# A new order of the prologue of an attention-plus-MLP kernel, and two pieces of h summed by TensorE

## The chip, the cores and the metric

The kernel runs on one core of one Trainium2 chip. The metric is the device time of one execution in microseconds (us): before the change a median of 589.53 us over 3 runs (589.42 to 589.62). Lower is better.

The engines are named as in the profile: PE is TensorE, DVE is VectorE, ACT is ScalarE, POOL is GpSimd and SP is SyncE, which issues DMAs here.

## The reference

```python
# x (4, 12480, 128), inducing (32, 128), w_in (128, 2048), w_out (2048, 128), alpha (2048)
def mab(q, kv):
    s = scale * (q @ kv.transpose(0, 2, 1))        # scale = 1 / sqrt(128)
    s = s - s.max(-1, keepdims=True)
    a = np.exp(s)
    a /= a.sum(-1, keepdims=True) + 1e-09
    return a @ kv
h = mab(I, x)                  # 32 inducing points look at the 12480 rows of a batch
y = mab(x, h)                  # each row looks at the 32 rows of h
...
hid = y.reshape(49920, 128) @ w_in
g = np.maximum(hid, 0.0) + alpha * np.minimum(hid, 0.0)
return g @ w_out
```

## The kernel before

The second attention and the MLP are folded: `g` is a relu part, whose weights are `W1 = w_out * (1 - alpha)`, and a linear part with a weight of its own, `Amat`. A *visit* handles 512 rows of x and 512 of the 2048 hidden columns in groups of matmuls: L855 multiplies the attention weights `a` of the rows by `HW = h @ w_in`, DVE (L870) and ACT (L868) take the relu into `gt`, and L881 multiplies `gt` by `W1`. Visits fill the program from the end of the prologue to its end. What DVE, ACT and POOL do beside them (the first attention of the next batches among it) is laid out by a planner with costs and due times, `Plan`.

The **prologue** is the first attention of batch 0, which nothing overlaps, since the first visit needs its h. It works on *pieces* of x, numbered 0 to 7: pieces 0 and 2 to 5 are loads of 1024 KB (16 tiles of 128 rows), piece 1 is the 192 rows that are left over, and pieces 6 and 7 are the two halves, 512 KB each, of the last 2048 rows. Its order is written out by hand, as one string of steps that are run from left to right; each engine's queue is in the order in which the steps issue to it. A step is a letter, a piece, a part after a point, and the engine as the last letter (p POOL, a ACT, v DVE):

- `k` casts a part of a load to bf16 (L353 on ACT, L355 on POOL and DVE), `t` transposes it on PE (L370), `c` copies the transposed tiles out of PSUM (L376 ACT, L378 DVE). When the last cast of a load has been issued, `load_next` sends the next load of x from SP.
- `s` are the scores against the inducing points on PE (L385), `m` their least value on DVE (L424; the scores carry a minus sign), `e` the exponentials on ACT (L450), `u` and `v` their transposition on PE (L488) and the copy back (L494 ACT, L496 DVE).
- `h` is a piece's share of h, summed in PSUM by PE (L505); `g` adds it to the running sum `hs` on DVE, pieces 1 to 3 with a factor `fac` (`f`, L468; L530), pieces 4 to 7 with a worth `ex` (L521).
- The tail: `ml` the lowest of all (`lo`, L399), `mg` (L549, ACT), `lz` (L406), `ex` (L584, ACT), `rb` on PE, `mm` (L565), `gs` scales `hs` (L412, POOL), `dx` and `dn` the denominator (L594, L597), `mf` the factors that join the four groups of partitions (L571), `pd` the denominator on PE (L614), `rec` its reciprocal (L619, L620), `ph` the sum of `hs` over the groups on PE (L629), `hT` the product (L634). Then `b` and the steps up to `ba` make the first attention weights `a` (L691 to L834), `w` and `hw` make `HW` (L645, L652), `kwp` casts w_in and `ww` makes `W1` and `AW` on POOL (L1137, L1021, L1030). `lw` loads w_in and w_out.
- `Z` and `W` are matmuls of blank tiles into a PSUM bank that nobody reads (L1007): one of 512 columns in f32, or so many of 256 columns in bf16.

A f32 matmul counts as several records in the profile. `al` is a small f32 transposition of alpha on PE (L1094).

Of the kernel before, what the change touches and what calls it, by code (L numbers as in the profile page):

```python
# [13 lines left out]
COPY = mybir.ActivationFunctionType.Copy  # L14
MULT = mybir.AluOpType.mult
# [6 lines left out]
P = 128  # L22
R = 4
# [3 lines left out]
EPS = 1e-9  # L27
# [3 lines left out]
def kernel(  # L31
# [9 lines left out]
    nc = tc.nc  # L41
    f32 = mybir.dt.float32
    bf16 = mybir.dt.bfloat16

    B, N, C = x.shape
    M = inducing.shape[0]
# [5 lines left out]
    scale = 1.0 / math.sqrt(C)  # L52
# [42 lines left out]
    const = ctx.enter_context(tc.tile_pool(name="const", bufs=1))  # L95
# [6 lines left out]
    sm_pool = ctx.enter_context(tc.tile_pool(name="sm", bufs=2))  # L102
# [11 lines left out]
    class Plan:  # L114
# [5 lines left out]
        COPY = {"a": 482, "v": 607}  # L120
# [164 lines left out]
    small = ring  # L285
# [9 lines left out]
    def new_state(b):  # L295
        st = State()
        st.b = b
        st.pieces = whole_pieces if b else first_pieces
        st.np = len(st.pieces)
        st.xT = xt_pool.tile([C, NT, P], bf16, name="xT", tag="xT")  # L300
        st.xn, st.xs, st.s1, st.e1T, st.e1, st.s1p, st.hp = {}, {}, {}, {}, {}, {}, {}
        st.e2, st.m2, st.den2, st.rc, st.rep = {}, {}, {}, {}, {}

        st.mx = sm_pool.tile([P, NX], f32, name="mx", tag="mx")
        st.rm = sm_pool.tile([P, NX], f32, name="rm", tag="rm")
        st.fac = sm_pool.tile([P, NX], f32, name="fac", tag="fac")
        st.da = sm_pool.tile([P, NX], f32, name="da", tag="da")
        st.ex = sm_pool.tile([P, NX], f32, name="ex", tag="ex")
        st.dx = sm_pool.tile([P, NX], f32, name="dx", tag="dx")
        st.lo = sm_pool.tile([P, 1], f32, name="lo", tag="lo") if not b else st.rm[:, st.np - 1 : st.np]  # L310
        st.den = sm_pool.tile([P, 1], f32, name="den", tag="den")
        st.hs = h_pool.tile([P, C], f32, name="hs", tag="hs")
        eng = nc.gpsimd if b else nc.vector
        eng.memset(st.mx[:], HIGH)
        eng.memset(st.da[:], 0.0)
        return st
# [198 lines left out]
    def a_add(st, pc):  # L515
# [22 lines left out]

        plan.then(work)

    def a_h_add(st, pc):
        a_h(st, pc)
        a_add(st, pc)

    def a_max(st):

        st.mg = sm_pool.tile([P, R], f32, name="mg", tag="mg")
        def work():
            nc.scalar.activation(  # L549
                out=st.mg[:], in_=group[:], func=COPY, scale=st.lo[:]  # L550
            )

        plan.then(work)

    def a_factors_pe(st):

# [52 lines left out]

    def a_den_pe(st):  # L610

        pd = small([P, M])
        den = st.den[:].broadcast_to([P, P])
        nc.tensor.matmul(pd[:], den, st.mf[:], start=True, stop=True)  # L614
        return pd

    def a_den_rec(st, pd):
        st.rec = sm_pool.tile([P, M], f32, name="rec", tag="rec")
        nc.vector.tensor_scalar(out=st.rec[:], in0=pd[:], scalar1=EPS, scalar2=None, op0=ADD)  # L619
        nc.vector.reciprocal(out=st.rec[:], in_=st.rec[:])  # L620

# [3 lines left out]

    def a_sum_pe(st):

        ph = small([P, M])
        nc.tensor.matmul(ph[:], st.hs[:], st.mf[:], start=True, stop=True)  # L629
        return ph  # L630

    def a_sum_div(st, ph):
        st.hT = hTs[st.b]
# [324 lines left out]
    st = new_state(0)  # L958
    xs_left = const.tile([P, supers[-1][1], C], f32, name="xs_left")
    for pc in first_pieces[:5]:  # L960
# [18 lines left out]
    mask = const.tile([P, M], f32, name="mask")  # L979
    nc.vector.tensor_reduce(  # L980
        out=mask[:], in_=ident32[:].rearrange("k (g m) -> k m g", g=R), axis=AX, op=ADD
    )
    group = const.tile([P, R], f32, name="group")
    nc.vector.tensor_reduce(
        out=group[:], in_=ident32[:].rearrange("k (g m) -> k g m", g=R), axis=AX, op=ADD
    )
    same = const.tile([P, R, M], f32, name="same")
    nc.vector.tensor_copy(out=same[:], in_=mask[:].unsqueeze(1).broadcast_to([P, R, M]))
    low = const.tile([P, M], f32, name="low")
    nc.vector.tensor_scalar(  # L990
        out=low[:], in0=mask[:], scalar1=-1.0, scalar2=HIGH, op0=ADD, op1=MULT
# [5 lines left out]
    W1 = const.tile([P, NK, C], bf16, name="W1")  # L997
# [72 lines left out]
    def load_next(done):  # L1070


        if not waiting:
            return
        for pc in waiting.pop(0):
            a_load(st, pc)
# [20 lines left out]
    def begin(step):  # L1097


        if step == "Z":  # L1100
            warm(blank, 1, BT * P)
            return
        if step[0] == "W":
            warm(blank_b, int(step[1:]), 2 * P)
            return
        plain = {
            "mg": lambda: a_max(st),
            "rb": lambda: kept.update(rb=a_factors_pe(st)),
            "mm": lambda: a_factors_min(st, kept["rb"]),
            "mf": lambda: a_factors_exp(st),  # L1110
            "ex": lambda: a_worth(st),
            "ml": lambda: a_lowest(st),
            "lz": lambda: a_from_lowest(st),
            "gs": lambda: a_scale(st),
            "lw": load_weights,
            "dx": lambda: a_weigh(st, nc.gpsimd),
            "dn": lambda: a_den_total(st),
            "ww": second_weights,
            "pd": lambda: kept.update(pd=a_den_pe(st)),
            "rec": lambda: a_den_rec(st, kept["pd"]),  # L1120
            "ph": lambda: kept.update(ph=a_sum_pe(st)),
            "hT": lambda: a_sum_div(st, kept["ph"]),
            "b": first_products,
            "bm": first_most,
            "bs": first_less,
            "be": lambda: b_exp_once(kept["be"], BT, w0[:, :BT]),
            "rx": rest_most,
            "rl": lambda: rest_less(BT, BT),
            "rk": lambda: rest_less(H, H),
            "re": lambda: rest_exp(BT, BT),  # L1130
            "bt": lambda: kept.update(bt=b_turn_pe(w0[:, :BT], BT)),
            "ba": lambda: b_turn_copy(st, 0, 0, BT, kept["bt"], False),
            "b2": lambda: b_products(st, 0, BT, ST - BT, later),
            "w": lambda: a_w(st),
            "al": lambda: kept.update(al=alpha_turn()),
            "alc": lambda: nc.vector.tensor_copy(out=alT[:], in_=kept["al"][:]),
            "kwp": lambda: nc.gpsimd.tensor_copy(out=w_in_b[:], in_=kept["w_in"][:]),  # L1137
            "om": lambda: nc.gpsimd.tensor_scalar(
                out=om_al[:], in0=alT[:], scalar1=-1.0, scalar2=1.0, op0=MULT, op1=ADD
            ),  # L1140
            "hw": lambda: a_w_copy(st),
            "hwv": lambda: a_w_copy(st, False),
        }
        if step in plain:
            plain[step]()
            return
        f, act = step[0], step[-1] == "a"
        p, _, part = step[1:].rstrip("avp").partition(".")
        pc = first_pieces[int(p)]
        if f in "tc":  # L1150
            t0, n = cuts[pc.n][int(part)]
            if f == "t":
                kept["t", p, part] = a_turn_pe(st, pc, t0, n)
            else:
                a_turn_copy(st, pc, t0, n, kept.pop(("t", p, part)), act)
        elif f == "k":
            a_cast_part(st, pc, *cuts[pc.n][int(part)], step[-1])
            done = first_pieces[int(p)].s
            if pc.full and step == last_cast[done]:
                load_next(done)  # L1160
        elif f == "u":
            kept["u", p] = a_e1_pe(st, pc)
        elif f == "v":
            a_e1_copy(st, pc, kept.pop(("u", p)), act)
        else:
            {"s": a_scores, "m": a_least, "e": a_exp, "f": a_fac, "h": a_h, "g": a_add}[f](st, pc)
# [5 lines left out]
    }  # L1172
    assert ST == 16 and NX == 8 and short[2] == 2
    order = """
        k0.0v k1.0p k0.1a k0.2a k2.0p Z t0.1 c0.1a t0.0 k2.2p t0.2 al k3.0p t1.0 c0.0v k2.1a
        c0.2v k3.1p Z s0 t2.1 c1.0a t2.0 alc m0 c2.0v t2.2 om c2.1v k4.0p s1 k5.2p m1 e0
        c2.2a k3.2a e1 f1 s2 t3.2 k5.0p m2 c3.2v u0 e2 t3.0 k6.0p u2 c3.0v v0v u1 v2v k4.1a
        k6.1p t3.1 t4.1 W2 t4.0 k4.2a c3.1v k7.1p f2 v1v t4.2 c4.1v c4.2v s3 m3 h0 c4.0a
        k5.1a W2 s4 e3 t5.2 g0 m4 h2 h1 g1 t5.1 t5.0 c5.2a W1 t6.0 g2 u3 k7.0p c5.1a c5.0v
        e4 W1 t6.1 s5 t7.1 v3v W1 t7.0 c6.0a c6.1v m5 f3 c7.0v s6 c7.1a m6 W2 s7 u4 e5 m7 u5  # L1180
        ml v4v e6 lw lz h3 mg ex u6 g3 v5v h4 gs e7 g4 rb dx u7 mm v6a h5 v7a mf dn h6 h7 g5
        g6 g7 pd W5 ph rec hT W4 b b2 kwp bm w bs rx be rl hw W3 bt ww ba re rk
    """
    waiting = [first_pieces[5:6], first_pieces[6:]]
    last_cast = {}
# [59 lines left out]
    first = {}  # L1245
# [61 lines left out]
    for b in range(B - 1):  # L1307
# [3 lines left out]
        for p, pc in enumerate(whole_pieces):  # L1311
# [18 lines left out]
            f = pc.full  # L1330
# [101 lines left out]
```

## Time and profile before

| what | value |
|---|---|
| median of 3 runs | 589.53 us (589.42 to 589.62) |
| the profiled execution | 591.3 us |
| its span in the profile | 589.2 us |
| PE, DVE, ACT, POOL busy | 580.1, 532.4, 538.1, 216.8 us |
| first visit begins (first L855) | 31.00 us |
| DMA moved | 80.55 MB |

The profiled execution took 2.1 us more than its span and 1.8 us more than the median. All times inside an execution below are of that one, in us from the start of its span.

### The profile page before, as it was taken

The page shows a single profiled execution, that of the slowest core. Times are in us where ns is not written, and L with a number is a line of the kernel's source. Part 1 is how long each engine was busy: PE and PEld are TensorE (multiplying, and loading weights), DVE is VectorE, ACT ScalarE, POOL GpSimd, SP SyncE. Part 2 cuts the span into 40 slices and gives each one's busy share as a digit, 9 for nine tenths or more (in the row PEclk, how much of TensorE's full clock was granted, in tenths as well). Part 3 has the DMA queues.
Part 4 walks back from the last instruction along what each step waited for, and adds up shares of the span by engine and source line. Part 5 has one row for each costly group of instructions (what it writes and reads, how often), then busy time and mean ns, then how long its engine had stood idle before and what let it go on. Part 6 is the DMA issues. An engine that isn't in the chain of part 4 may idle for free.

```text
span 589.2 us, 22996 instructions
## 1 busy us (share of the span) xinstructions
PE 580.1 (98%) x9443; PEld 436.6 (74%) x9443; DVE 532.4 (90%) x968; ACT 538.1 (91%) x1091; POOL 216.8 (37%) x259
## 2 busy tenths in 40 slices
PE   8899999999999999999999999999999999999997
PEld 3677777777777777777777777777777777777776
DVE  5799998998999999899999999999999999999995
ACT  5699999999999999999999999998998998999886
POOL 3575543523325517313226346133143143143110
PEclk9999999999999999999999999999999999999999
DMA  8687699634188799332256899641341331432321
GB/s 332 249 214 180 164 216 221 148 66 91 38 240 186 185 210 222 100 90 57 83 152 186 183 229 241 135 100 38 92 78 52 92 80 50 118 82 61 91 68 49
DMA packets 121962, 80.55 MB, mean 137 GB/s; under 512 B 103760, under 2 KB 105728, under 8 KB 118784
## 3 DMA queue, kind: packets, MB, share of 16 engines
q1 hardware_dynamic: 121632, 78.99, 55.5%
q8 instruction: 74, 1.21, 0.8%
q14 instruction: 32, 0.26, 0.1%
q10 hardware_dynamic: 224, 0.09, 0.1%
HBM read 28.07 MB, written 25.56 MB: 91 GB/s over the span
## 4 chain that ended last, share of the span: by engine, by line
PE 95%; DMA 3%; POOL 1%; DVE 0%; issue 0%; SPq 0%; ACT 0%; DVEq 0%; POOLq 0%
PE bp L881 66%; PE hh L855 22%; DMA xs<-in_x_dram 3%; PE bp L908 2%; PE hh L691 2%; PE hh L505 1%; PE hh L385 1%; POOL xn L355 0%; PE bp L1007 0%; PE hh L645 0%; PE hh L614 0%; PE hh L629 0%; PE hh L1040 0%; PE hh L826 0%; SPq L326 0%
## 5 line engine op out<-in xcount | busy, mean ns | idle before, releaser
L870 DVE TENSOR_SCALAR gt<-hh 128x512 bf16<-128x512 f32 x726 | 465.2, 684 | 29.5 <-PE hh L855 15.9
L868 ACT ACTIVATE gt<-hh 128x512 bf16<-128x512 f32 x834 | 448.3, 615 | 32.4 <-PE hh L855 27.4
L881 PE MATMUL bp<-W,gt 128*128 128x128 bf16 x6240 | 416.4, 220 | 0.0
L881 PEld LDWEIGHTS <-gt 128*128 128x128 bf16 x6240 | 349.4, 98 | 82.2 <-issue 75.1
L855 PE MATMUL hh<-a,HW 32*128 32x512 bf16 (+2 forms) x1664 | 154.1, 371 | 0.5 <-DVE a L834 0.5
L805 POOL TENSOR_TENSOR rep<-e,rc 128x2048 bf16<-128x2048 f32 (+2 forms) x26 | 84.8, 3264 | 19.9 <-DVE rc L796 19.5
L759 POOL TENSOR_TENSOR t<-e 128x256 f32<-128x256 f32 (+1 forms) x24 | 17.2, 717 | 186.8 <-ACT e L735 186.8
L855 PEld LDWEIGHTS <-HW 32*128 32x128 bf16 x1664 | 40.2, 91 | 41.6 <-issue 5.6
L773 POOL TENSOR_TENSOR e<-e,smx 128x512 f32<-128x512 f32 (+1 forms) x24 | 24.6, 1024 | 112.9 <-DVE smx L768 112.9
L934 ACT COPY ob<-bp 128x512 f32<-128x512 f32 (+1 forms) x89 | 53.0, 596 | 2.8 <-PE bp L881 0.5
L759 POOL TENSOR_TENSOR t<-t 128x128 f32<-128x128 f32 (+3 forms) x100 | 30.3, 303 | 7.8
L338 POOL CAST xn<-xs 128x2048 bf16<-128x2048 f32 x17 | 32.1, 1889 | 1.6 <-DMA xs<-in_x_dram 0.7
L424 DVE TENSOR_SCALAR_CACHE_REDUCE s<-hh 128x512 f32<-128x512 f32 (+2 forms) x29 | 18.0, 619 | 2.8 <-PE hh L385 2.5
L908 PEld LDWEIGHTS <-a 32*128 32x128 bf16 x392 | 15.0, 93 | 5.9 <-issue 0.2
L450 ACT ACTIVATE e1T<-s,rm 128x512 bf16<-128x512 f32 (+1 forms) x25 | 18.4, 735 | 1.1 <-DVE rm L434 1.0
L908 PE MATMUL bp<-HA,a 32*128 32x128 bf16 x392 | 19.1, 214 | 0.0
L768 DVE TENSOR_REDUCE smx<-e 128x16 f32<-128x512 f32 (+1 forms) x24 | 15.9, 662 | 0.0
L735 ACT ACTIVATE e<-e 128x512 f32<-128x512 f32 (+1 forms) x24 | 15.4, 640 | 0.0
L749 ACT COPY e<-hh 128x512 f32<-128x512 f32 (+1 forms) x22 | 13.5, 612 | 0.0
L691 PE MATMUL hh<-hT,xT 128*128 128x32 bf16 x372 | 13.0, 176 | 0.0
L691 PEld LDWEIGHTS <-xT 128*128 128x128 bf16 x384 | 12.1, 96 | 0.2
L530 DVE SCALAR_TENSOR_TENSOR hs<-hs,fac,hh 128x128 f32<-128x128 f32 (+1 forms) x21 | 7.2, 345 | 5.3 <-PE hh L505 4.3
(117 smaller groups left out, 188.7 us busy)
## 6 DMA issues: line engine op xcount, KB each, us to landing
out_dram<-ob SPq DMA_DIRECT2D x97, 256.0 KB, 2.4
xs<-in_x_dram SPq DMA_DIRECT2D x23, 1024.0 KB, 6.4
xs<-in_x_dram SPq DMA_DIRECT2D x2, 512.0 KB, 8.4
w_in_f<-in_moe_w_in_dram SPq DMA_DIRECT2D x1, 1024.0 KB, 10.1
a<-rep SPq DMA_TRANSPOSE x27, 4.6
xs_left<-in_x_dram SPq DMA_DIRECT2D x4, 96.0 KB, 5.9
xT<-xn SPq DMA_TRANSPOSE x18, 6.1
e<-e1T SPq DMA_TRANSPOSE x18, 3.2
```

The costliest lines, as they stand in the source:

```text
L338: nc.gpsimd.tensor_copy(out=st.xn[s][:], in_=xs[:])
L450: nc.scalar.activation(out=e1T[:parts, : pc.q * P].rearrange("m (j t) -> m j t", j=pc.q)[:, :, : pc.last], in_=s1[:parts, :cols].rearrange ...
L691: nc.tensor.matmul(ps[w, t, :], st.xT[:, tile0[s] + t, w], hTs[b][:], start=True, stop=True)
L759: nc.gpsimd.tensor_tensor(out=t[:, :n], in0=src[:, :n, :w], in1=src[:, :n, w : 2 * w], op=ADD)
L773: nc.gpsimd.tensor_tensor(out=st.e2[s][:, :n], in0=st.e2[s][:, :n], in1=st.m2[s][:, :n].unsqueeze(2).broadcast_to([P, n, M]), op=SUB,)
L805: nc.gpsimd.tensor_tensor(out=st.rep[s][:, ts], in0=st.e2[s][:, ts].unsqueeze(2).broadcast_to([P, n, R, M]), in1=rc[:, ts].unsqueeze(2).un ...
L855: nc.tensor.matmul(hh[:, q * cols + w.start : q * cols + w.stop], HWs[b][rows, v * P : (v + 1) * P], a2[rows, t0 : t0 + nt, :].rearrange(" ...
L868: nc.scalar.activation(out=gt[:, :cols], in_=hh[:, :cols], func=RELU)
L870: nc.vector.tensor_relu(gt[:, :cols], hh[:, :cols])
L881: nc.tensor.matmul(blk.acc[:, t * C : (t + 1) * C], gt[:, (q * nt + t) * P : (q * nt + t + 1) * P], W1[:, k, :], start=(not blk.begun), st ...
L908: nc.tensor.matmul(blk.acc[w, t * C : (t + 1) * C], blk.a2[rows, blk.t0 + t, w], HAs[b][rows, :], start=(not blk.begun and t == 0), stop=F ...
L934: nc.scalar.copy(out=ob[:, :nt], in_=acc)
```

## The change

Only the prologue changes: what an engine runs behind it has the same order as before. The string of steps is new as a whole; the diff gives both in full. Lines of the changed kernel have numbers of their own, since it is longer.

- The f32 blank matmul ahead of the first transposition is gone (`Z` ahead of `t0.1`), and `al` stands in its place with two short bf16 ones (`W2`) behind the first part; the two `Z` now stand ahead of `s0` and ahead of `k4.1p`. One `W1` is new at the very end.
- Casts are dealt out anew among POOL, ACT and DVE.
- `mg` is made on POOL (`mgp`), where ACT made it. The order of `ex` and `e7` on ACT is turned round.
- The small constant in the denominator, which an instruction on DVE added (L619), is added by a matmul of a new constant tile `eps` into the denominator's PSUM tile (`pz`), ahead of time; the reciprocal then reads PSUM.
- Pieces 6 and 5 are no longer added to `hs` on DVE. Each is multiplied by its worth into a tile of its own (`G6v` on DVE, `G5a` on ACT), and PE adds these tiles in f32 to the sum over the groups (`q6`, `q5`).

```diff
+    def a_weighted(st, pc, act):
+        ps = st.hp.pop(pc.k)
+        st.hw[pc.k] = sm_pool.tile([P, C], f32, name=f"hw{pc.k}", tag=f"hw{pc.k}")
+        worth = st.ex[:, pc.k : pc.k + 1]
+        if act:
+            nc.scalar.activation(out=st.hw[pc.k][:], in_=ps[:], func=COPY, scale=worth)
+        else:
+            nc.vector.tensor_scalar(
+                out=st.hw[pc.k][:], in0=ps[:], scalar1=worth, scalar2=None, op0=MULT
+            )
...
+    def a_max_pool(st):
+        st.mg = sm_pool.tile([P, R], f32, name="mg", tag="mg")
+        nc.gpsimd.tensor_scalar(
+            out=st.mg[:], in0=group[:], scalar1=st.lo[:], scalar2=None, op0=MULT
+        )
...
     def a_den_pe(st):
-        pd = small([P, M])
+        first = st.pd is None
+        if first:
+            st.pd = small([P, M])
         den = st.den[:].broadcast_to([P, P])
-        nc.tensor.matmul(pd[:], den, st.mf[:], start=True, stop=True)
-        return pd
+        nc.tensor.matmul(st.pd[:], den, st.mf[:], start=first, stop=True)
+        return st.pd
+
+    def a_den_eps(st):
+        st.pd = small([P, M])
+        nc.tensor.matmul(st.pd[:], eps[:].broadcast_to([P, P]), mask[:], start=True, stop=False)
 
     def a_den_rec(st, pd):
         st.rec = sm_pool.tile([P, M], f32, name="rec", tag="rec")
+        if not st.b:
+            nc.vector.reciprocal(out=st.rec[:], in_=pd[:])
+            return
...
     def a_sum_pe(st):
-        ph = small([P, M])
-        nc.tensor.matmul(ph[:], st.hs[:], st.mf[:], start=True, stop=True)
-        return ph
+        a_sum_part(st, st.hs, True)
+        return st.ph
+
+    def a_sum_part(st, hs, last):
+        first = st.ph is None
+        if first:
+            st.ph = small([P, M])
+        nc.tensor.matmul(st.ph[:], hs[:], st.mf[:], start=first, stop=last)
...
+    eps = const.tile([P, 1], f32, name="eps")
+    nc.vector.memset(eps[:], EPS / R)
...
+        elif f == "q":
+            a_sum_part(st, st.hw.pop(pc.k), False)
+        elif f == "G":
+            a_weighted(st, pc, act)
...
-        k0.0v k1.0p k0.1a k0.2a k2.0p Z t0.1 c0.1a t0.0 k2.2p t0.2 al k3.0p t1.0 c0.0v k2.1a
-        c0.2v k3.1p Z s0 t2.1 c1.0a t2.0 alc m0 c2.0v t2.2 om c2.1v k4.0p s1 k5.2p m1 e0
-        c2.2a k3.2a e1 f1 s2 t3.2 k5.0p m2 c3.2v u0 e2 t3.0 k6.0p u2 c3.0v v0v u1 v2v k4.1a
-        k6.1p t3.1 t4.1 W2 t4.0 k4.2a c3.1v k7.1p f2 v1v t4.2 c4.1v c4.2v s3 m3 h0 c4.0a
-        k5.1a W2 s4 e3 t5.2 g0 m4 h2 h1 g1 t5.1 t5.0 c5.2a W1 t6.0 g2 u3 k7.0p c5.1a c5.0v
-        e4 W1 t6.1 s5 t7.1 v3v W1 t7.0 c6.0a c6.1v m5 f3 c7.0v s6 c7.1a m6 W2 s7 u4 e5 m7 u5
-        ml v4v e6 lw lz h3 mg ex u6 g3 v5v h4 gs e7 g4 rb dx u7 mm v6a h5 v7a mf dn h6 h7 g5
-        g6 g7 pd W5 ph rec hT W4 b b2 kwp bm w bs rx be rl hw W3 bt ww ba re rk
+        k0.0a k0.1v k0.2p al k1.0p k3.0p t0.1 W2 t0.2 c0.1v k2.1a t0.0 alc c0.2v c0.0v k2.0v
+        t1.0 k3.1p Z k4.0p k2.2a s0 t2.0 m0 c1.0a t2.1 c2.0v c2.1a Z k4.1p s1 e0 t2.2 m1
+        c2.2v s2 e1 k5.2p u0 m2 u1 t3.0 k5.0p t3.1 k3.2a t3.2 c3.0v v0v v1a f1 c3.1v t4.0
+        k4.2v t4.1 e2 c4.0v f2 c3.2a u2 t4.2 v2v c4.1a h0 s3 g0 t5.2 c4.2a m3 lw h1 k6.0p
+        k6.1p s4 k5.1a g1 t5.1 t5.0 k7.0p h2 c5.2a e3 c5.1a t6.0 m4 e4 c5.0v f3 t6.1 s5 u3
+        g2 k7.1p c6.0a om c6.1v t7.0 t7.1 m5 W1 c7.0v s6 v3a c7.1v W1 u4 e5 s7 m6 h3 W2 W2
+        e6 u6 m7 ml u5 v4v mgp g3 lz e7 rb ex v6v u7 pz mm h6 v5a v7v gs G6v dx dn h4 mf h5
+        g4 h7 pd G5a g7 kwp q6 rec q5 ph hT W3 b bm ww b2 bs W5 w rx be hw rl re bt W4 ba rk
+        W1
```

The first place is the start of PE's queue, behind the jump into the program. `blank` and `ind_b` are the blank tile and the inducing points, `al_f` is alpha, `xn` the cast x. In the kernel before:

```order
L1007 MATMUL bp<-blank 128x512 x2
L1011 LDWEIGHTS ind_b
L1011 MATMUL hh<-ident,ind_b 128x32
L1007 MATMUL bp<-blank 128x512
L370 LDWEIGHTS xn
```

In the changed kernel:

```order
L1044 MATMUL bp<-blank 128x512 x2
L1048 LDWEIGHTS ind_b
L1048 MATMUL hh<-ident,ind_b 128x32
L1131 MATMUL hh<-ident_129,al_f 128x16
L371 LDWEIGHTS xn
```

The third f32 blank matmul is gone from between the inducing points and the first transpositions of x, and alpha's transposition has come in its place.

The second place is around PE's 190th instruction, counted as the profile counts them. In the kernel before it lies in the transpositions of piece 4, here with the tiles' numbers:

```order
L370 LDWEIGHTS xn_261
L370 MATMUL hh_337<-ident_151,xn_261 128x128
L370 LDWEIGHTS xn_261
L370 MATMUL hh_352<-ident_151,xn_261 128x128
L370 LDWEIGHTS xn_261
```

In the changed kernel it lies where the transpositions of the exponentials of piece 2 (`e1T`) end:

```order
L489 LDWEIGHTS e1T_338
L489 MATMUL hh_343<-ident_151,e1T_338 128x128
L371 LDWEIGHTS xn_229
L371 MATMUL hh_348<-ident_151,xn_229 128x128
L371 LDWEIGHTS xn_229
```

What stands there now needs the exponentials of piece 2 to be done, where before it needed only casts of x.

The third place is the end of h on DVE: `hs` is the running sum, `hw` the tile of piece 6, `m` and `den` the two small reductions of the tail. In the kernel before:

```order
L521 TENSOR_SCALAR hs<-hh,ex,hs 128x128
L565 TENSOR_REDUCE m_584<-hh 128x1
L597 TENSOR_REDUCE den<-dx 128x1
L521 TENSOR_SCALAR hs<-hh,ex,hs 128x128 x3
L619 TENSOR_SCALAR rec<-hh 128x32
L620 RECIPROCAL rec<-rec 128x32
L634 TENSOR_TENSOR hT_139<-hh,rec 128x32
```

In the changed kernel:

```order
L584 TENSOR_REDUCE m_566<-hh 128x1
L497 COPY e_579<-hh 128x256
L550 TENSOR_SCALAR hw_582<-hh,ex 128x128
L616 TENSOR_REDUCE den<-dx 128x1
L522 TENSOR_SCALAR hs<-hh,ex,hs 128x128 x2
L646 RECIPROCAL rec<-hh 128x32
L669 TENSOR_TENSOR hT_139<-hh,rec 128x32
```

Four additions to `hs` have become two and one product into a tile of its own, and the addition of the constant ahead of the reciprocal is gone.

More of the change, by code (lines that the diff above doesn't have):

```diff
@@ L302, in new_state @@
         st.e2, st.m2, st.den2, st.rc, st.rep = {}, {}, {}, {}, {}
+        st.hw, st.ph, st.pd = {}, None, None
         st.mx = sm_pool.tile([P, NX], f32, name="mx", tag="mx")
@@ L1106, in begin @@
         plain = {
-            "mg": lambda: a_max(st),
+            "mgp": lambda: a_max_pool(st),
             "rb": lambda: kept.update(rb=a_factors_pe(st)),
@@ L1118, in begin @@
             "ww": second_weights,
+            "pz": lambda: a_den_eps(st),
             "pd": lambda: kept.update(pd=a_den_pe(st)),
```

## The prediction, made before the changed kernel was run

> **What bounds the kernel now.** I read the page first: the share of the engines and the chain that ended last.
>
> ```profile
> PE 580.1 (98%) x9443; PEld 436.6 (74%) x9443; DVE 532.4 (90%) x968; ACT 538.1 (91%) x1091; POOL 216.8 (37%) x259
> ...
> PE 95%; DMA 3%; POOL 1%; DVE 0%; issue 0%; SPq 0%; ACT 0%; DVEq 0%; POOLq 0%
> ```
>
> The end is set by PE for 95% of the span and by DMA for 3%. The table by stages says where which holds (per engine: busy time and number of instructions):
>
> ```profile
> 9.00:12.00 3.00, 2.77 (x23) 1.19 (x23) 1.95 (x7) 1.63 (x5) 1.59 (x2) 1.00 1.01 421
> 12.00:16.00 4.00, 3.05 (x40) 2.22 (x40) 3.83 (x14) 3.74 (x11) 2.81 (x4) 1.00 1.01 420
> 16.00:19.50 3.50, 3.50 (x75) 2.51 (x73) 3.19 (x12) 2.97 (x6) 2.33 (x4) 1.00 1.05 421
> 19.50:22.60 3.10, 1.70 (x23) 1.04 (x21) 1.97 (x6) 1.79 (x6) 1.55 (x3) 1.00 0.98 345
> ...
> 60.00:560.00 500.00, 500.00 (x8157) 379.72 (x8152) 462.45 (x816) 470.06 (x951) 181.96 (x205) 1.00 0.56 129
> ```
>
> From 60 to 560 us PE is never idle. This work is not touched, so it can only begin earlier or later, and the change is worth what it moves the first visit. The chain of waits up to there, in order of time (start, length, what), has these pieces:
>
> ```profile
> 11.68 9.69 DMA xs<-in_x_dram
> ...
> 21.42 1.18 POOL xn L355 x2
> ...
> 24.46 0.17 DVE lo L399
> ...
> 26.72 0.33 ACT mf L571
> ...
> 27.10 0.41 PE hh L614 x2
> ...
> 28.05 0.34 PE hh L629 x2
> ...
> 29.64 0.43 PE bp L1007 x3
> 30.52 0.44 DVE a L834
> ...
> 31.00 0.37 PE hh L855
> ```
>
> So the prologue is the load of x, up to 21.37 (11.68 and 9.69), then a tail of 9.6 us from the casts of piece 7 to the first visit at 31.00. POOL's casts show when the loads came; in brackets is the idle time and its releaser:
>
> ```profile
> 9.68 1.59 POOL L355 CAST xn<-xs 128x1024 bf16<-128x1024 f32 x2 [1.83 <-DMA xs<-in_x_dram]
> 12.18 1.60 POOL L355 CAST xn<-xs 128x1024 bf16<-128x1024 f32 x2 [0.90 <-DMA xs<-in_x_dram]
> ...
> 14.67 1.04 POOL L355 CAST xn<-xs 128x1024 bf16<-128x1024 f32 x1 [0.72 <-DMA xs<-in_x_dram]
> 17.17 2.71 POOL L355 CAST xn<-xs 128x512 bf16<-128x512 f32 x4 [1.46 <-DMA xs<-in_x_dram]
> 21.42 1.17 POOL L355 CAST xn<-xs 128x512 bf16<-128x512 f32 x2 [1.54 <-DMA xs<-in_x_dram]
> ```
>
> A load of 1024 KB came every 2.5 us (9.68, 12.18, 14.67, 17.17). Two loads of 512 KB follow, which at that pace are there at 18.42 and 19.67. The second was there at 21.42: **1.75 us late**. The DMA queues of 19.2 to 20.4 us, the page's sum of one of them, and PE's instructions up to 16.21 us show what came in between:
>
> ```profile
> q1 hardware_dynamic: 61, 0.49, 100.9%
> q8 instruction: 1, 0.02, 5.8%
> ...
> q8 instruction: 74, 1.21, 0.8%
> ...
> 0.00:16.21 16.21, 13.54 (x93) 6.78 (x93) 9.02 (x33) 8.85 (x20) 5.49 (x13) 1.00 0.86 337
> ```
>
> PE has 9443 + 9443 = 18,886 instructions; over 74 packets that is 255, so q8 carries PE's instructions in blocks of 256. The one packet in this stretch is the first, and by 16.21 PE had begun 93 + 93 = 186 instructions: the 190th, about, asks for it, and it goes through from 19.2 on, 3 us later, over the end of the load. I read the late landing as this collision: one DMA engine that carries the packet (5.8% of 16 engines over 1.2 us is 1.1 us of one) finishes its share of the load late, and the load counts as landed when the last share has. That is inferred from one execution; 0.65 of the 1.75 us it does not explain.
>
> **The change, part by part.** *The collision.* The 190th instruction now stands behind the transposition of piece 2's exponentials, which come off a chain of casts, scores and ACT. I estimate it at 16.6 to 16.8, half a us later, from the spacing of 2.5 us of the loads that this chain hangs on. A packet asked for at 16.7 goes through at about 19.7 with the same lag of 3 us: just behind the load's last packets, into the load of w_in. That one is not urgent: its cast stands at 26.28 on POOL, as the next rows show. If the load lands at 19.67, the casts of piece 7 can start 1.75 earlier. What is late next is PE: between 17 and 22.6 it idles this long for those casts (busy and mean | idle and its releaser):
>
> ```profile
> L370 PE MATMUL hh<-ident,xn 128*128 128x128 bf16 x28 | 2.4, 220 | 1.4 <-POOL xn L355 1.4
> ...
> 26.28 1.89 POOL L1137 CAST w_in_b<-w_in_f 128x2048 bf16<-128x2048 f32 x1
> ```
>
> PE's order needs all it does there, so the gain is between 0 (the packet still meets the load) and 1.4; since DVE and ACT have similar gaps in that stretch (1.97 and 1.79 busy of 3.10) I take 1.3.
>
> [...]
>
> *The end of h.* On DVE and ACT, before:
>
> ```profile
> 26.66 1.26 DVE L521 SCALAR_TENSOR_TENSOR hs<-hh,ex,hs 128x128 f32<-128x128 f32 x3
> 27.84 0.18 DVE L619 TENSOR_SCALAR rec<-hh 128x32 f32<-128x32 f32 x1
> 28.06 0.35 DVE L620 RECIPROCAL rec<-rec 128x32 f32<-128x32 f32 x1
> 28.52 0.19 DVE L634 TENSOR_TENSOR hT<-hh,rec 128x32 bf16<-128x32 f32 x1
> ...
> 27.10 0.41 PE L614 MATMUL hh<-mf,den 128*128 128x32 f32 x2 [0.37 <-ACT mf L571]
> ```
>
> Two of the additions go (1.26 / 3 = 0.42 each, 0.84 in all), and the 0.18 of L619. But `mf` is ready only at 26.72 + 0.33 = 27.05, and everything behind it remains: the denominator on PE until 27.51, two more f32 pairs for `q6` and `q5` (0.41 each until visible, less when they follow one another: I take 0.24), and the sum of `hs` (0.34 to 0.41). That is 27.10 + 3 x 0.24 + 0.41 = 28.23 for PE's sum against 28.39 before (28.05 + 0.34); the reciprocal, 27.55 to 27.90, lies beside it. So of 0.84 + 0.18 about 0.15 to 0.3 is left, in front of `hT`. On ACT the two operations behind `lo` stood so:
>
> ```profile
> 24.66 0.30 ACT L549 ACTIVATE mg<-group,lo 128x4 f32<-128x4 f32 x1 [0.17 <-DVE lo L399]
> 24.86 0.29 ACT L584 ACTIVATE ex<-rm,lo 128x8 f32<-128x8 f32 x1
> ```
>
> With `mg` on POOL, ACT saves the 0.2 between these two starts, and `ex` behind `e7` loses about as much, since `e7` can begin before `lo` is there; I take 0, with 0.2 either way. The new `W1` ahead of the first visit waits for the blank matmuls before it and costs 0.14 to 0.28 (0.43 / 3 for one, above, or two) if `a` is ready by then. Sum of the tail: -0.27 + 0.14 = **-0.13**, between -0.3 and +0.2.
>
> *The start of PE.* Here the change takes cover away:
>
> ```profile
> 1.45 3.78 PE L1007 MATMUL bp<-blank 128*128 128x512 f32 x4 [1.45 <-DVE blank L957]
> ...
> 5.37 2.08 PE L1007 MATMUL bp<-blank 128*128 128x512 f32 x2
> 7.49 1.12 PE L370 MATMUL hh<-ident,xn 128*128 128x128 bf16 x16
> ...
> 8.83 1.08 PE L1007 MATMUL bp<-blank 128*128 128x512 f32 x2
> ...
> L967 ACTq DMA_DIRECT2D al_f<-in_moe_alpha_dram x1: 440/440/440, 1.2 to 1.2; - x1
> ...
> DMA to landing us min/median/max: 6.0/6.0/6.0
> ```
>
> The same blank matmul took 1.04 us a half at 5.37 (2.08 / 2) and 0.54 at 8.83: PE's real speed doubled between, although the clock column above reads 1.00 throughout. PE had worked without a break since 1.45. Now the matmul at 5.37 is gone, and `al` must wait for alpha, which lands at 1.2 + 6.0 = 7.2. PE therefore stands still from 5.44 to about 7.2. If the doubling is already earned by the 4.0 us of work from 1.45, or by work that adds up across the gap (the remaining 1 to 3.4 us then end at 8.2 to 10.6), PE's later idle time, 0.23 and 0.95 in the two stretches from 9 to 16, pays for it: 0. If the gap starts it anew, the 5 to 7.4 us run from 7.2 and end at 12.2 to 14.6; this is the second rival.
>
> [...]
>
> Redistributed casts and the two `Z` further back are priced at 0: the loads set the pace there, and POOL waited for each of them (0.72 to 1.83 above). If that cover fails, a `Z` costs its 1.08 once.
>
> **The rivals.** *First: the load is held up all the same* (the packet lags by less than I think, or goes in at the end of the load all the same, or the late landing had another cause). For it: a shift of 0.5 against a lag of which I have one value. Then only the tail is left, -0.13: 589.4. The change then doesn't do what it says, since the 190th instruction is later without effect.
>
> *Second, on the other side: PE reaches full speed only at 12.2 to 14.6*, because of the gap from 5.44 to 7.2. At half speed PE does half its work; from 7.6, where it ran fast before, to the middle, 13.4, that is 5.8 / 2 = 2.9 us left undone. Of that the idle 1.18 could be regained, but ACT's and DVE's casts stand in one queue with copies that wait for PE, so the loads behind them slide as well: I take 0.2 regained. -1.43 + 2.7 = +1.3: 590.8, and from -1.43 + 1.7 = +0.3 to -1.43 + 3.4 = +2.0 at the ends. It decides from about 11.5 on: there 3.9 / 2 = 1.95 less some 0.5 equals the gain.
>
> *Third: full speed at about 10.6 to 11.5.* It eats what the load gives: (11 - 7.6) / 2 = 1.7 less some 0.4 regained, -1.43 + 1.3 = -0.1: 589.4.
>
> **How the numbers follow.** Forecast: -1.3 - 0.13 = -1.43. The profiled execution (591.3, of which 2.1 around the span of 589.2) would be 589.9; it stands 1.8 above the median of the runs shown, so against that median 589.53 - 1.43 = 588.1. A measurement of this kernel tells about 0.2%, 1.18 us, from no change: below 588.35 is faster, above 590.71 slower. Chances: the collision goes and the clock costs nothing 0.42 (588.1; 587.8 to 588.4 by the bounds of 1.4 and the tail); first rival 0.13 and third 0.12 (both 589.4, within 0.2%); second 0.33 (590.8). That the collision goes I give 0.75, since with the same lag the packet comes half a us behind the place where it met the load; the clock's gap is close to even. The range reaches from 587.8 to 591.2, which leaves out the upper third of the second rival and a little below.
>
> **What would show it.** In the changed profile: the casts of piece 7 on POOL at about 19.7 instead of 21.42 and q8's first packet behind the load; the first L855 at about 29.6; the start of `hT` about 0.2 nearer to `mf`. Blank or score matmuls at double length after 11 would show the second rival, casts of piece 7 again at 21 the first. The forecast is wrong if the first visit is not earlier than 30.

## The result, and the profile after

The changed kernel is slightly **slower**: a median of 590.45 us over 21 runs against 589.42 over 21 runs of the kernel before, 1.03 us more. Over all runs the ratio is 1.0024 (95% interval 1.0015 to 1.0032): the interval leaves out no change, but 1.03 us is less than the 1.18 us that the prediction took as its limit for calling it slower. Its runs also spread far more, 588.93 to 594.84 against 588.94 to 589.80. The profiled execution took 590.46 us with a span of 588.4, so this time it stands at its own median. That of the kernel before took 591.3: none of its 21 runs came near that.

POOL's casts of x, and the first visit on PE, in the changed kernel (start, length, both in us):

```profile
14.17 1.60 POOL L356 CAST xn<-xs 128x1024 bf16<-128x1024 f32 x2 [0.83 <-DMA xs<-in_x_dram]
16.60 4.02 POOL L356 CAST xn<-xs 128x512 bf16<-128x512 f32 x6 [0.83 <-DMA xs<-in_x_dram]
...
29.93 0.40 PE L890 MATMUL hh<-a,HW 32*128 32x512 bf16 x4
```

From 16.60 on POOL casts without a break to 20.62: the last load no longer keeps it waiting (it landed at 19.27 by the trace's DMA records, before at 21.37). The first visit is 1.07 us earlier than in the profile of before, 29.93 against 31.00. But the last load is 2.10 earlier; 1.03 is lost on the way. The start of PE and the stages around it (granted clock third from the right) show where:

```profile
6.98 0.20 PE L1131 MATMUL hh<-ident,al_f 16*128 16x16 f32 x1 [1.63 <-DMA al_f<-in_moe_alpha_dram]
...
8.35 1.85 PE L1044 MATMUL bp<-blank 128*128 128x512 f32 x2
...
11.93 1.08 PE L1044 MATMUL bp<-blank 128*128 128x512 f32 x2
...
7.00:9.00 2.00, 2.00 (x22) 1.52 (x23) 1.43 (x4) 0.62 (x1) 0.81 (x2) 0.88 1.01 426
9.00:10.50 1.50, 1.50 (x6) 0.11 (x4) 0.82 (x2) 1.21 (x3) 0.00 (x0) 0.50 1.00 426
10.50:12.00 1.50, 1.50 (x17) 1.33 (x14) 1.11 (x4) 0.20 (x1) 0.26 (x1) 0.52 1.04 437
```

PE waits 1.63 us for alpha. The clock, which had risen early (the trace's record has it full from 5.10), falls back to half from 8.52 to 11.93, and the blank matmul at 8.35 takes 1.85 where the one at 11.93 takes 1.08. The end of h:

```profile
26.09 0.38 PE L635 MATMUL hh<-mf,den 128*128 128x32 f32 x2
26.31 0.61 PE L665 MATMUL hh<-mf,hw 128*128 128x32 f32 x4
26.75 0.39 PE L665 MATMUL hh<-mf,hs 128*128 128x32 f32 x2
...
27.18 0.19 DVE L669 TENSOR_TENSOR hT<-hh,rec 128x32 bf16<-128x32 f32 x1 [0.26 <-PE hh L665]
```

From the denominator's matmul to `hT` it is now 27.18 - 26.09 = 1.09 us; before it was 28.52 - 27.10 = 1.42. Further on, a part of this is given back. Two pieces of the chain of waits just ahead of the first visit, and the copy of `a` that the visit needs:

```profile
29.73 0.27 PE bp L1044
30.00 0.33 PE hh L890 x4
...
29.19 0.42 DVE L869 COPY a<-hh 128x512 bf16<-128x512 bf16 x1
```

`a` is done at 29.61, but the visit's first matmul starts at 29.93, 0.32 us later, and the new `W1` (the piece at 29.73) stands in between. In the four profiled executions with before's tail this distance is 0.05 us, in all ten with the new tail 0.32 or 0.33. So `W1` costs about 0.27 by this reading; no run leaves it out alone.

And there is one place, far behind the prologue, that the prediction did not look at. The waits of PE from 32 us to the end have a line, and DVE and PE at 126 us look so:

```profile
PE hh L577 <- DVE gt L905: 0.2, 1, 0.2
...
126.01 1.89 DVE L905 TENSOR_SCALAR gt<-hh 128x512 bf16<-128x512 f32 x3 [0.39 <-ACT gt L903]
...
126.76 0.39 PE L577 MATMUL hh<-mg,same 128*128 128x4 f32 x2 [0.19 <-DVE gt L905]
```

Laid visit by visit beside an execution of the kernel before (base_again, below), PE keeps a constant distance to 127 us, then loses 0.35 us in one step, then keeps its distance to the end.

One table for what follows, from the profiled executions: when the last of the 16 shares of the last load of x landed (the trace records 16 landings of a load), when the trace's clock record shows PE at full speed, the first visit and its distance to that landing, and the time from the first L881 (L916) to the start of PE's last matmul.

| execution | time | load landed | full clock from | first visit | distance | rest |
|---|---|---|---|---|---|---|
| before | 591.30 | 21.37 | 7.64 | 31.00 | 9.63 | 552.51 |
| base_again | 589.62 | 19.69 | 4.83 | 29.31 | 9.63 | 552.51 |
| before_without_Z | 589.09 | 19.16 | 5.58 | 28.81 | 9.65 | 552.51 |
| before_fetch_early | 589.67 | 19.11 | 5.03 | 28.74 | 9.62 | 553.15 |
| before_with_new_tail | 590.19 | 20.38 | 6.53 | 29.73 | 9.36 | 552.80 |
| new_tail_and_dve | 589.47 | 19.83 | 5.73 | 29.18 | 9.36 | 552.54 |
| after | 590.46 | 19.27 | 5.10 to 8.52, and 11.93 | 29.93 | 10.66 | 552.87 |
| after_again_1 | 590.83 | 19.03 | 10.88 | 30.30 | 11.27 | 552.86 |
| after_again_2 | 589.13 | 19.13 | 5.51 | 28.50 | 9.36 | 552.89 |
| after_again_3 | 589.66 | 18.74 | 9.62 | 29.10 | 10.36 | 552.80 |
| after_with_Z | 590.40 | 20.55 | 6.52 | 29.92 | 9.36 | 552.83 |
| after_and_dve | 589.82 | 20.17 | 4.41 | 29.57 | 9.40 | 552.50 |
| after_with_Z_and_dve | 588.70 | 19.11 | 5.64 | 28.50 | 9.39 | 552.54 |
| after_cold | 591.18 | 19.25 | 11.71 | 30.59 | 11.34 | 552.83 |

### The profile page after: what moved, and what is told of

Its sections match the earlier page's. It is cut to its first block, busy times and chain, and to the rows that moved or that the text cites. A ratio compares the mean times of both kernels' runs of the same rounds, so it can differ in the third digit from the quotient of the medians.

```text
span 588.4 us, 23006 instructions
## 1 busy us (share of the span) xinstructions
PE 580.0 (99%) x9449; PEld 437.3 (74%) x9449; DVE 532.7 (91%) x968; ACT 537.9 (91%) x1090; POOL 217.0 (37%) x260
## 4 chain that ended last, share of the span: by engine, by line
PE 95%; ACT 1%; issue 0%; DVE 0%; ACTq 0%
PE bp L916 66%; PE hh L890 22%; PE bp L943 2%; PE hh L726 2%; PE hh L506 1%; PE hh L386 1%; ACT gt L903 1%; PE bp L1044 0%; PE hh L680 0%; PE hh L665 0%; PE hh L577 0%; PE hh L489 0%; PE hh L635 0%; PE hh L1077 0%; DVE gt L905 0%
## 5 line engine op out<-in xcount | busy, mean ns | idle before, releaser
L916 PE MATMUL bp<-W,gt 128*128 128x128 bf16 x6240 | 416.3, 220 | 0.0
L916 PEld LDWEIGHTS <-gt 128*128 128x128 bf16 x6240 | 349.3, 98 | 82.2 <-issue 75.1
L356 POOL CAST xn<-xs 128x512 bf16<-128x512 f32 (+1 forms) x11 | 8.1, 766 | 10.9 <-DMA xs<-in_x_dram 10.9
```

Source lines behind the costliest of these rows:

```text
L916: nc.tensor.matmul(blk.acc[:, t * C : (t + 1) * C], gt[:, (q * nt + t) * P : (q * nt + t + 1) * P], W1[:, k, :], start=(not blk.begun), st ...
```

## The experiments

The medians and ratios to the kernel before (11 runs each, the kernel before 15 to 33 on the same chip; its median there was 589.30, 589.35 or 588.94, so medians of different rows can differ by some 0.4 us before any edit, and the ratios are the safer comparison). The edits below show only the part of a line that differs.

| kernel | median | range | ratio (95%) |
|---|---|---|---|
| before_without_Z | 590.45 | 589.09 to 591.21 | 1.0018 (1.0009 to 1.0026) |
| before_with_new_tail | 589.09 | 588.73 to 590.19 | 0.9999 (0.9990 to 1.0008) |
| new_tail_and_dve | 588.61 | 588.40 to 589.64 | 0.9992 (0.9983 to 1.0001) |
| before_fetch_early | 589.67 | 588.82 to 592.37 | 1.0009 (0.9999 to 1.0020) |
| after_with_Z | 589.71 | 588.79 to 590.97 | 1.0004 (0.9995 to 1.0013) |
| after_and_dve | 589.42 | 588.43 to 590.58 | 1.0003 (0.9994 to 1.0012) |
| after_with_Z_and_dve | 589.17 | 588.49 to 589.85 | 0.9995 (0.9986 to 1.0004) |
| after_cold | 590.75 | 589.77 to 591.18 | 1.0020 (1.0011 to 1.0029) |

**Is the late load the rule?** (base_again: the kernel before, no edit.)

> The kernel before, unchanged, profiled once more. Theory (the profiled execution of before, 1.8 us above its own median, was the odd one: its last load of x was late, and ordinary executions have it in time): the casts of piece 7 begin at about 19.7, the first visit at 29.2 to 29.6, and the time is 589.2 to 589.8. Rival (the load is late in every execution): casts of piece 7 at 21.4 again, first visit at 31.0, and the execution near 591.3.

POOL's casts and the first visit of this second profile of the kernel before:

```profile
14.34 1.04 POOL L355 CAST xn<-xs 128x1024 bf16<-128x1024 f32 x1 [0.73 <-DMA xs<-in_x_dram]
16.85 4.06 POOL L355 CAST xn<-xs 128x512 bf16<-128x512 f32 x6 [1.47 <-DMA xs<-in_x_dram]
...
29.31 0.40 PE L855 MATMUL hh<-a,HW 32*128 32x512 bf16 x4 [0.53 <-DVE a L834]
```

No wait of POOL for the last load, and the first visit at 29.31, at 589.62 us. The two executions differ by 1.68 us in time, by 1.68 in the landing of the load (21.37 and 19.69) and by 1.69 in the first visit: the late load is the whole difference. The odd execution was the one that the prediction was read from; that it was the packet which made the 16th share late (15 of 16 had landed by 19.41, the last at 21.37) stays an inference from that one. A late share needs no packet: in base_again, too, the last share came 0.74 us behind the 15th (19.69 and 18.95), and the packet began only at 19.86.

**The gap on PE, from both sides.** after_with_Z puts the blank matmul back, before_without_Z takes it out of the kernel before:

```diff
-        k0.0a k0.1v k0.2p al k1.0p
+        k0.0a k0.1v k0.2p Z al k1.0p
```

> The changed kernel with the f32 blank matmul put back ahead of alpha's transposition, so that PE works without a gap from 1.45 to about 7.4. Theory (PE's clock falls back or rises late because of the gap from 5.3 to 7.0, in a way that differs from execution to execution): the spread of 588.9 to 594.8 shrinks to under 1 us and the median falls from 590.45 to 588.3 to 589.0. Rival (the new order and dealing out of the casts are slower by themselves): the median stays within 0.5 us of 590.4.

```diff
-        k0.2a k2.0p Z t0.1
+        k0.2a k2.0p t0.1
```

> The kernel before without its f32 blank matmul ahead of the first transposition, nothing else changed. Theory (the gap on PE): the runs spread over 2 to 6 us and the median rises by 0.7 to 2 us above the kernel before. Rival (the gap is harmless, the new order costs the time): median within 0.3 us of the kernel before, spread as before.

With the blank matmul the changed kernel's median falls by 0.74 us and its highest run from 594.84 to 590.97; without it the kernel before loses 1.15 us (590.45 against 589.30) and spreads over 2.1 us. So the gap costs, in either order. Putting it back did not reach 588.3 to 589.0, and the runs still spread over 2.2 us, not under 1: the median was too high by 0.7, of which DVE's step, below, is about 0.35. The profiled execution of before_without_Z was its fastest run and had the clock early (5.58), so in that kernel the late clock was not seen in a trace; it is argued from the changed kernel. In the profiled execution of after_with_Z the loads were slow besides, with packets of 8 KB taking 342 ns where the others' took 309 to 313.

**Does the clock do it, execution by execution?** (after_again_1 to 3: the changed kernel, no edit.)

> The changed kernel, unchanged, profiled again, to see its clock in another execution. Theory (PE's clock goes by windows of 3.4 us that start at another moment in each execution, and the gap on PE spoils one of them in some): other edges of the clock than 5.10, 8.52 and 11.93 us, and a first visit that goes with them: about 28.7 where full speed holds from about 5 us on, 29.9 where it falls back or comes at 10.5 to 12, later than 30.5 where it comes after 13. Rival (the spread comes from the loads alone): the clock's edges stand where they stood, and the first visit follows the landing of the last load.

> The changed kernel profiled a third time, with the same expectations as the second time: by the theory other edges of the clock, and a first visit that goes with them; by the rival the same edges, and a first visit that follows the last load.

> The changed kernel profiled a fourth time, with the same expectations as the second time: by the theory other edges of the clock, and a first visit that goes with them; by the rival the same edges, and a first visit that follows the last load.

The f32 blank matmul behind the first transpositions and the first visit, one pair of rows for each of the three in turn:

```profile
8.94 2.02 PE L1044 MATMUL bp<-blank 128*128 128x512 f32 x2
...
30.30 0.39 PE L890 MATMUL hh<-a,HW 32*128 32x512 bf16 x4
```

```profile
7.66 1.08 PE L1044 MATMUL bp<-blank 128*128 128x512 f32 x2
...
28.50 0.39 PE L890 MATMUL hh<-a,HW 32*128 32x512 bf16 x4
```

```profile
8.68 1.55 PE L1044 MATMUL bp<-blank 128*128 128x512 f32 x2
...
29.10 0.40 PE L890 MATMUL hh<-a,HW 32*128 32x512 bf16 x4
```

The same program, three speeds of the same matmul: 2.02, 1.08 and 1.55 us. By the table, full speed holds from 10.88, 5.51 and 9.62, and the distance from load to first visit is 11.27, 9.36 and 10.36, at landings within 0.4 us of one another. The rival, the loads, is out: the latest of the three landings has the earliest visit. Over the four executions of the changed kernel the clock cost 1.30, 1.91, 0 and 1.00 against 9.36, 1.05 in the mean. The mean granted clock that is on record for every run hints at how often it falls back: the profiled execution with its 3.41 us of half speed (half of it is 0.003 of the span) has 0.997, and 8 of the changed kernel's 21 runs have 0.997 or less, against 1 of the 75 runs of the kernel before beside the experiments.

**The clock late for certain.** (after_cold, which leaves out only blank matmuls.)

```diff
-    warm(blank, 2, BT * P)
```

> The changed kernel without the two f32 blank matmuls at the very start, so that PE has no work before 5.2 us that could raise its clock early. Theory (the clock's rise decides): every run has the rise at 10.4 to 14.1, the median is 591 to 592.5, above the 590.45 of the changed kernel. Rival (the clock is not what costs the time): within 0.4 us of 590.45.

The median is 590.75, 0.3 above the changed kernel, so by my own numbers the rival's forecast held and the theory's did not. The test told less than I thought, since the changed kernel itself has its clock late in three of its four profiled executions. The profile, with full speed from 11.71 and a distance of 11.34, is the theory's case, 2 us more than with an early clock. What it does tell is that even 590.75 and a highest run of 591.18 are far from 592.9 to 594.8, where three of the changed kernel's 21 runs lay. None of those was profiled. Their granted clocks on record, 0.995, 0.997 and 0.997, would fit a fall back to half speed after a first rise, as the profile with 0.997 had it; after_cold, which has no early rise to lose, has no run below 0.999. But five runs with 0.997 took only 590.26 to 590.49, so what cost the three another 2.5 to 4.4 us stays open.

**The new tail alone** (the order of before up to the scores of piece 7, then the changed kernel's tail; the edit was made to the changed kernel and is shown against before's order):

```diff
         m6 W2 s7 u4 e5 m7 u5
-        ml v4v e6 lw lz h3 mg ex u6 g3 v5v h4 gs e7 g4 rb dx u7 mm v6a h5 v7a mf dn h6 h7 g5
-        g6 g7 pd W5 ph rec hT W4 b b2 kwp bm w bs rx be rl hw W3 bt ww ba re rk
+        ml v4v e6 lw u6 mgp h3 g3 lz e7 rb ex v6v u7 pz mm h6 v5a v7v gs G6v dx dn h4 mf h5
+        g4 h7 pd G5a g7 kwp q6 rec q5 ph hT W3 b bm ww b2 bs W5 w rx be hw rl re bt W4 ba rk
+        W1
```

> The order of before up to the scores of piece 7, and the tail of the changed kernel behind it: worth products of pieces 6 and 5 summed by PE, the constant by PE, the lowest's spread on POOL, one blank matmul at the end. Theory (the tail alone gains): 0.3 to 0.9 us faster than before, 588.5 to 589.1, with before's small spread. Rival (the tail's gain was given back, as the prediction had it with -0.13): within 0.2 us of before.

A ratio of 0.9999: by the time alone the rival. But the profile has two changes of opposite sign: the distance falls from 9.63 to 9.36, and the rest grows from 552.51 to 552.80, in one step at 176.6 us, where DVE starts late:

```profile
175.85 1.29 DVE L905 TENSOR_SCALAR gt<-hh 128x512 bf16<-128x512 f32 x2 [0.54 <-ACT ob L969]
```

That step is the next experiment's.

**DVE's step.** At both steps (127 us in the changed kernel, 176.6 us here) the instruction of DVE that starts late is record 319 and record 447 of its queue (counted from 0): 5 x 64 - 1 and 7 x 64 - 1. The change takes DVE from 1500 records to 1497, and the new tail to 1498, so that behind the prologue other instructions stand at these numbers. Small memsets of a constant that is written anyway bring the count back to 1500, three for the changed kernel and two here:

```diff
     nc.vector.memset(eps[:], EPS / R)
+    nc.vector.memset(eps[:], EPS / R)
+    nc.vector.memset(eps[:], EPS / R)
+    nc.vector.memset(eps[:], EPS / R)
```

> The changed kernel with the blank matmul put back, and three more memsets of the constant tile eps on DVE at the start, so that DVE runs 1500 instructions as before the change and not 1497. Theory (DVE starts one instruction some 0.35 us late at the end of each block of 64; after the change such a place stands where PE waits, at 127 us, and PE loses 0.35 us there): the step at 127 us is gone, PE runs from the first L916 to the end in 556.6 us as before, and the median is 0.35 us under the 589.7 of the kernel without the memsets: 589.3 or less. Rival (the step comes from the order of something else): 556.9 from the first L916 to the end, median 589.7.

> The order of before with the new tail, and two more memsets of eps on DVE, again 1500 instructions. Theory: the step of 0.31 us at 176.6 us is gone, 556.6 us from the first L916 to the end, and the median falls from 589.1 to 588.7 to 588.9, faster than before by 0.4 to 0.6. Rival: no change against the kernel without the memsets, 589.1.

> The changed kernel with the three memsets on DVE alone, its gap at the start of PE left as it is. Theory (gap and DVE's step are two costs that add): 0.35 to 0.5 us under the changed kernel, 589.9 to 590.1 in the median, with its wide spread, and 0.5 to 0.9 us above the same kernel with the blank matmul put back. Rival (the blank matmul was what took the step away, and the gap costs nothing): 589.2.

PE and DVE at the same place as above in after_with_Z_and_dve:

```profile
124.98 0.39 PE L577 MATMUL hh<-mg,same 128*128 128x4 f32 x2
125.30 0.39 PE L890 MATMUL hh<-a,HW 32*128 32x512 bf16 x4
...
123.52 2.61 DVE L905 TENSOR_SCALAR gt<-hh 128x512 bf16<-128x512 f32 x4
```

The step is gone in all three: the rest is 552.54, 552.54 and 552.50, as before the change (552.51), against 552.80 to 552.89 in the seven executions of the new tail without them. The profile had named a result of ACT as what DVE waited for at 126.01; with nothing changed on ACT the wait is gone, so it was not that.

Laid record by record beside one another, executions with 1497, 1498 and 1500 records show more: behind the prologue the only steps of DVE over 0.25 us are single starts that come 0.35 to 0.37 late, at records 319, 447, 702 or 703, 959 and 1087, whatever instruction stands there. They are in the kernel before as well (319 and 703 in base_again), where other work covers them; the change moved a result that PE waits for onto one. (The 556.6 and 556.9 expected count to PE's very last record; the difference of 0.3 is the same.)

The medians fell by 0.54, 0.48 and 1.03. The first two are as forecast within 0.2; the third fell further than theory had it: 589.42 lies nearer to the rival's 589.2 than to 589.9 to 590.1, on a chip where the kernel before is 0.48 lower too. Between the kernels with and without the blank matmul the two ratios, 1.0003 and 0.9995, leave 0.47 us, just under the 0.5 to 0.9 that I gave, and their intervals overlap. Full speed came from another moment in each profiled execution, so eleven runs are too few to put the gap's price closer than 0.5 to 1.2 us; that it and the step are two costs is shown by the traces, not by these medians.

**A packet that is asked for earlier** (before_fetch_early):

```diff
-        c0.2v k3.1p Z s0 t2.1
+        c0.2v k3.1p W8 s0 t2.1
...
-        c3.2v u0 e2 t3.0
+        c3.2v W4 u0 e2 t3.0
```

> The kernel before with its second f32 blank matmul replaced by eight bf16 ones and four more of them ahead of the transposition of piece 0's exponentials, so that PE's 190th instruction comes 20 records, about 0.5 us, earlier, at 15.3 to 15.7. Theory of the collision (PE's packet meets the last load of x if it is asked for some 3 to 4 us ahead of that load's end): more runs lose 0.7 to 1.7 us, two groups of runs, median 0.3 to 1.5 us above before. Rival (a packet on the load's engine does no harm, or meets it just as rarely as before): within 0.2 us of before, one group.

Inconclusive: a ratio of 1.0009 that just includes 1, and one run at 592.37 that was not profiled; its granted clock, 0.993, is the lowest of all, which speaks for the clock rather than for the packet. PE's 190th instruction came at 14.74 in the profile, 1.6 us earlier than in the profile of before (16.32) and not the 0.5 that I had reckoned with, and the packet at 19.09 instead of 19.22; the load was in time (19.11). So the packet does not follow that instruction by a fixed 3 us. In the eight executions of the table where the 190th came between 14.74 and 16.32 the packet was served between 19.05 and 19.86, in the other six, where it came between 16.43 and 18.52, between 19.79 and 20.48. That an early one waits in the queue until about the end of the last load fits these times, but is not shown; nor is that the 190th instruction is the one that asks. Here a stall of another kind, 0.60 us at 223 us, went into the rest; the one wait of PE behind 32 us that its profile lists is 0.4 us, for a transposition by DMA:

```profile
PE hh L385 <- DMA xT<-xn: 0.4, 1, 0.4
```

## Why the prediction was wrong

The range, 587.8 to 591.2, holds the time; the sign is wrong. Step by step:

- **What bounds the kernel**: right. Every execution is the prologue and then a PE that hardly waits; the rest differs by 0.4 us at most, but for the one stall at 223 us.
- **The collision (-1.3)** is the step that failed. Its mechanism may be right for the execution that I read, but that execution was not the kernel: at 589.62 the kernel before has its load in time, and of the 15 to 33 runs of it beside each experiment none is above 590.24. The prediction even had the number: the profiled execution stood 1.8 us above the median, and the late load was 1.75 late. These are the same 1.8 us. A cost that only the profiled execution paid cannot be saved from the median, so the term is 0 there. Nor did the 190th instruction move as reckoned: with an early clock it came at 15.73 (after_again_2), not at 16.6 to 16.8, against 15.95 in base_again, and the packet does not follow it at a fixed lag anyway; that this instruction asks for the packet was my estimate, and no run shows it.
- **The tail (-0.13, between -0.3 and +0.2)**: right in kind and within its range, twice as large. The distance from load to first visit went from 9.62 to 9.65 in four executions of before's tail to 9.36 to 9.40 in all six of the new one with an early clock, -0.26. Both of its terms were about twice what the sum had: the `W1` cost 0.27, the upper end of the 0.14 to 0.28 that I gave, and the rest of the tail gained 0.53 instead of 0.27.
- **The start of PE (0, or the second rival)**: the gap that the second rival names did cost, but at another size. I gave it 0.33 and +1.7 to +3.4, with full speed from 12.2 to 14.6; three of four profiled executions of the changed kernel pay 1.00 to 1.91, with full speed from 9.62, 10.88 and (for good) 11.93. At 9.62 and 10.88, where the forecast and the third rival had 0 to 1.3, it cost 1.00 and 1.91. That the second rival's 590.8 lies near the measured 590.45 is luck: it has a gain of 1.3 in it that was not there, and a clock too dear by more than that. In the trace of the changed kernel the clock's edges at 5.10, 8.52 and 11.93 are 3.41 us apart, and where full speed first begins differs from execution to execution (4.41 to 11.71 in the table); what sets that moment, and whether earlier work adds up across a gap, no run shows.
- **Not in the sum at all: DVE's 0.35.** I took the program behind the prologue as a rigid block because its order is the same. It is, but with three DVE records fewer, the places at which DVE starts late fall on other instructions, one of which PE waits for.

The sum, mended: tail -0.26, DVE's step +0.35, the clock +1.05 in the mean of four executions, the collision 0: +1.14. Measured are +1.03 between the medians and +1.35 between the means (590.75 and 589.40), which the three highest runs draw up; four executions are too few for a closer agreement to be more than chance.

The version with the new tail on the old order and 1500 DVE records is the best here: 588.61, a ratio of 0.9992 (0.9983 to 1.0001), which just misses being told from no change; its profile has the shorter distance, 9.36, and before's rest, 552.54.

## What to carry to other kernels

Compare the profiled execution's time with the median before costing anything from it: if it stands apart by as much as a wait in it, that wait is probably the difference (here 1.8 us and 1.75), and removing it gains nothing in the median. Blank work at the start of PE is not filler: here, where it did not reach to the first real matmul, full speed held for good only from 9.62, 10.88 and 11.93 us on in three of four profiled executions of the changed kernel, and its runs spread over 5.9 us where those of the kernel before spread over 0.9. Code that is only shifted, not reordered, can still lose time: here 0.35 us, where DVE's late start, which stayed with the record's number, fell on a result that PE waits for.

## What the runs showed of the hardware

The clock's record of the changed kernel's profile has two entries of 3.41 us, full speed from 5.10 and half speed from 8.52, ahead of full speed for good from 11.93. PE was busy for all 3.41 us ahead of 5.10, for 1.79 of the 3.42 ahead of the fall at 8.52, and again for all 3.41 ahead of 11.93. In the profile of the kernel before, whose record has full speed from 7.64, it was busy for 3.36 of the 3.41 us ahead. So a rise stood behind 3.4 us of nearly unbroken work in these two profiles and the fall behind a stretch that was half idle; how much work a rise takes, the two do not show. Every other execution of the table has one rise in the prologue, so the windows of 3.4 us in the expectation for after_again_1 rest on the two entries of this one profile, and what happens at them in other executions stays my estimate. In the profile's table the clock column reads 1.00 also ahead of the first entry of the clock's record: in after_again_1, where the blank matmul at 8.94 ran at half speed, the stage from 9 to 10.5 us reads

```profile
9.00:10.50 1.50, 1.50 (x4) 0.38 (x2) 1.26 (x2) 1.06 (x3) 0.00 (x0) 1.00 1.02 431
```

so the length of a matmul of known size is the better witness. DVE's late start of about 0.35 us was seen at five places (records 319, 447, 702 or 703, 959 and 1087), each an odd multiple of 64 less one, or next to it; PE waited for it at two places, 127 and 176.6 us. It does not come ahead of every multiple of 64, as the expectation for after_with_Z_and_dve had it: at record 255 of the changed kernel DVE started 0.05 us after what it waited for, at record 319 it was 0.40. What makes DVE late at these records no run shows.
